# Attention output kept channel-major up to the output product, in a two-part transformer block on one core

## The chip, the cores and the metric

The kernel is one program on one core of a Trainium2 chip. The metric is the device time of a run in microseconds. Three runs of the kernel before gave 793.11, 795.96 and 798.07 us; the time before is their median, 795.96 us.

## What is computed

The block has two residual parts on a sequence of 2048 tokens with 512 channels, all in float32. `mod` is a row of six vectors computed from a condition `c`.

```python
h = layernorm(x) * (1 + ca) + sa
x = x + ga * A(h)
h = layernorm(x) * (1 + cb) + sb
x = x + gb * B(h)

# A: 32 heads of 16 channels, 4 segments of 512 tokens, causal inside a segment
a_dot = softmax(q k^T / 4 + mask) v
a_mem = (phi(q) M) / (phi(q) z + 1e-6)      # M, z: sums over the segments before
o = g * a_mem + (1 - g) * a_dot             # g = sigmoid(beta), one number a head
A = o @ wo
# B: relu(h @ w1 + b1)^2 @ w2 + b2, 1792 hidden channels
```

In the first segment M and z are zero, so its memory part is zero.

## The kernel before

**Units.** Attention is cut into 16 units: unit u is segment s = u // 4 and channel group cc = u % 4, that is 8 heads by 512 tokens. `qk` (L726) makes q and k of a unit, SP copies them into the operand tile ST (`fill`, L797: 12 DMAs a unit), `a_quad` (L850) finds row maxima for 4 heads at a time and SP writes them into ST (`rows`, L933), `b_quad` (L1019) makes the scores, the exponentials and the product with V. `mem` (L941) reads the memory M for segments 1 to 3 and adds to it for segments 0 to 2.

**What leaves a unit.** The product with V leaves each group of four heads in a PSUM bank as channel-major rows: 32 rows a head, of which 16 are channels and the 17th is the softmax denominator (V has a column of ones), by 512 tokens. ScalarE copies each of the two banks of a unit to `oraw` (L1110). `turn_o` (L1117) then turns them on TensorE with 2 x 8 transposes of 64x128 blocks, in two halves with a GpSimd memset between them as a hinge. `norms` (L1135) divides by the denominator and gates by 1 - g on VectorE, token-major. `mem` does the same for the memory part: 8 small products of phi(q) with M (L954), then a gate on VectorE (L957). The sum of both is made on GpSimd (on VectorE in the last segment, L1157). Segments 0 to 2 store it to `o_dram` (L1160); the last segment leaves it in SBUF, in X1L.

**Output product.** `wo_tile(g, ...)` (L1200) handles 128 tokens: it loads the rows of `o_dram` (the last segment reads X1L), turns them back to channel-major with 4 transposes on TensorE (L1219), splits the result in a high part (ScalarE, L1225) and a low part (VectorE, L1227), both out of PSUM, and does 4 steps of 3 matmuls each with `wo` (L1192 to L1194). The residual is added on VectorE (L1234).

**Second part.** `ffn1` and `ffn2` (L1348, L1378) run per segment over 14 blocks of 128 hidden channels. Their weights are loaded and split only when the SBUF of the attention part is free (`open_ffn`, L1300, `load_w1`, `load_w2`). The 16 output tiles are stored by SP (L1396), the last half tile by ScalarE's queue.

**Order.** Nothing is scheduled on the chip. Every operation is a node of a plan, numbered in the order in which the code makes it, and `ORDER` (L57 to L214) holds the node numbers of PE, ACT, DVE, POOL and SP in the order in which each engine runs them. An engine takes its list strictly in turn, and SP issues its DMAs strictly in turn: a DMA whose data isn't ready holds all DMAs behind it in the list. `Plan.run` models durations and ends at the end of TensorE's last node (L374), which is what the lists were made against. The SP list of before ends like this:

```
2710 2735 2696 2728 2717 2738 2731 2724 3162 2957 3575 3373 3364 3367 3168 2963 2960 3569 3370 3159 3578 3165 3572
2954
```

The last 16 are the stores of the output tiles. 2954 to 2963 belong to segment 0, 3159 to 3168 to segment 1, 3364 to 3373 to segment 2 and 3569 to 3578 to segment 3, so the third store of the list is one of segment 3.

Of the kernel before, what the change touches and what calls it, by code (L numbers as in the profile page):

```python
# [8 lines left out]
F32 = mybir.dt.float32  # L9
# [9 lines left out]
P = 128  # L19
# [12 lines left out]
VROW = NB * VA  # L32

# [25 lines left out]
16 48 32 25 76 42 68 73 54 50 19 74 46 56 80 45 69 63 3 77 31 78 40 29 65 62 24 36 17 22 59 47 41 66 71 79 51 43-44 57  # L59
82 21 84 94 102 26 61 96 104 113-114 58 30 125 38 81 126 49 83 67 27 70 35 28 33 72 23 85 178-179 64 39 168 180-181  # L60
169-172 182-183 18 184 173 60 174 75 175 185 34 20 52 55 37 53 333-336 204 338-339 205-206 238 246 207 340 248 341
209-212 257 490-491 243 492-493 270 749-750 495-496 251 759-760 497-498 221-223 276 224 262 253 226 265 227 362
228-229 267 614 281 615 288 291 616 272 617 375 296 619 284 620 381 386 621-622 372 370 300 304 279 301-302 311 367
314 307 391 433 319 377 389 394 519 404 323 436 324-325 438 445 396 406 527 538 412 327 448 767 329 768 441 769-770
532 453 551 772-773 557 548 774-775 524 529 420 457 560 458-459 422 414 461 546 464 428 468 872 471 934-935 534 476
936 543 937 643 656 430 480-482 562 648 939 569 940 681 941 651 942 565 800-801 577 802 553 803 572 484 805-806 486
807 662 808 581 653 585 582-583 592 675 658 588 600 670 595 1344-1345 1354-1355 667 684 604-606 672 686 1005 834 1067
693 1068 696 1069 677 1070 701 847 608 1072 610 689 1073 853 1074 844 1075 875 842 705-707 709 817 712 818 839 819 716
820 866 719 822 861 823 849 724 824 967 825 858 975 728-729 863 881 888 730 878 1200 980 868 1201 972 986 1202-1203
994 884 1205 1138 891 896 1206-1208 977 900 904 991 982 1100 1108 907 901 732 911 734 914 902 1113 919 923 1008 999  # L70
# [1363 lines left out]
```

## Time and profile before

| | |
|---|---|
| time, median of 3 runs | 795.96 us (793.11 to 798.07) |
| profiled execution, its own time | 798.18 us |
| profiled execution, span of the trace | 796.3 us |
| granted TensorE clock, mean | 0.989 |
| attention part | up to about 463 us of the span |
| second part on TensorE | 463 to 784 us |

The span runs from the first to the last instruction of the trace. A row of a timeline gives start and duration in microseconds, engine, line, operation and tile, "output<-input", and the count of instructions that the row merges; in brackets stands idle time before it and what ended it. PE's matmuls overlap, so the time that a group costs TensorE is the distance from its start to the start of the next row, not its duration. SPq is SP's sequencer, which issues DMAs; ACTq is that of ScalarE. A row of a stage table gives for each engine its busy time and count of instructions, then the granted clock as a fraction of the full one, the mean busy share of the 16 DMA engines, and GB/s.

### The profile page before, as it was taken

Reading aid. Unit: us, or ns where it says so; the run is one execution under the profiler, and the core shown is the slowest. Engines: PE = TensorE matmul, PEld = TensorE weight load, DVE = VectorE, ACT = ScalarE, POOL = GpSimd, SP = SyncE. Lnnn points to the kernel's source line nnn. Section 1 sums busy time; section 2 is a strip of 40 time slices with the busy share of each in tenths; the row PEclk is TensorE's granted clock in tenths of the full one; section 3 lists DMA queues with packets and bytes.
Section 4 is the critical chain, followed back from the end, with each engine's and each line's share of the span. In section 5 each row is a group of like instructions: output and inputs, shape, how many; then the busy total and the mean of one; then the engine's idle time right before and its main releaser. Section 6 shows DMA issues by size and latency. Waiting matters only on the chain.

```text
span 796.3 us, 16568 instructions
## 1 busy us (share of the span) xinstructions
PE 769.0 (97%) x6075; PEld 577.9 (73%) x6075; DVE 528.2 (66%) x1493; ACT 430.6 (54%) x908; POOL 222.1 (28%) x334
## 2 busy tenths in 40 slices
PE   8999999999999999999999999999999999999993
PEld 4776657775778658685676678888888888888883
DVE  4777688888998887689798878676522342323232
ACT  2568568879778885779647545433322232222130
POOL 1746454456655784344232200000000000000000
PEclk9999899999999999999999999999999999999998
DMA  8845652333333342453531254320000000000005
GB/s 270 244 102 128 185 178 52 82 82 82 95 91 85 83 95 63 100 119 116 160 102 41 82 147 119 97 62 1 0 1 1 0 27 1 1 0 1 0 1 184
DMA packets 51306, 65.33 MB, mean 82 GB/s; under 512 B 7829, under 2 KB 24985, under 8 KB 51226
## 3 DMA queue, kind: packets, MB, share of 16 engines
q1 hardware_dynamic: 51074, 64.14, 28.9%
q8 instruction: 48, 0.79, 0.4%
q14 instruction: 32, 0.26, 0.1%
q10 hardware_dynamic: 152, 0.13, 0.1%
HBM read 29.91 MB, written 7.34 MB: 47 GB/s over the span
## 4 chain that ended last, share of the span: by engine, by line
PE 66%; ACT 3%; DVE 2%; DMA 2%; SPq 1%; issue 1%; POOL 0%; DVEq 0%; POOLq 0%; ACTq 0%
PE bh L1357 6%; PE bh L1356 6%; PE bh L1358 6%; PE bpf L1385 6%; PE bpf L1386 6%; PE bpf L1384 6%; PE bqk L744 5%; PE bpv L1086 5%; PE bpb L1027 4%; PE ba L857 3%; PE bv L824 3%; ACT pt L1044 2%; PE bwop L1192 2%; PE bwop L1194 2%; PE bwop L1193 1%; PE blnq L606 1%
## 5 line engine op out<-in xcount | busy, mean ns | idle before, releaser
L862 DVE CUSTOM_DVE_ANT_0 ba<-ba,msk 128x384 f32<-128x384 f32 (+2 forms) x384 | 186.3, 543 | 31.2 <-PE ba L857 26.1
L1044 ACT ACTIVATE pt<-bpb 128x512 f32<-128x512 f32 x320 | 173.6, 614 | 30.8 <-PE bpb L1027 29.0
L1373 DVE TENSOR_TENSOR r<-r 128x512 f32<-128x512 f32 x56 | 38.7, 692 | 136.9 <-ACT rr L1370 136.7
L744 PE MATMUL bqk<-HT,WQK 64*128 64x512 f32 x720 | 102.5, 398 | 1.1 <-ACT phi L790 1.1
L1031 POOL TENSOR_SCALAR_AFFINE_SELECT pt<-pt 128x512 f32<-128x512 f32 x128 | 80.4, 646 | 82.9 <-ACT pt L1044 62.8
L1366 ACT ACTIVATE r<-bh,b1c 128x512 f32<-128x512 f32 x56 | 38.5, 688 | 109.6 <-DVE rr L1374 56.5
L1384 PE MATMUL bpf<-W,rr 128*128 128x512 f32 x224 | 88.1, 393 | 0.0
L1385 PE MATMUL bpf<-W,rr 128*128 128x512 f32 x224 | 87.8, 392 | 0.0
L1386 PE MATMUL bpf<-W,rr 128*128 128x512 f32 x224 | 87.7, 392 | 0.0
L1027 PE MATMUL bpb<-ST 64*128 64x256 f32 (+2 forms) x512 | 80.6, 356 | 2.6 <-DMA ST<-mt 1.3
L1086 PE MATMUL bpv<-pt,VT 128*32 128x512 f32 (+3 forms) x1024 | 81.2, 441 | 0.2
L857 PE MATMUL ba<-ST 63*128 63x256 f32 (+2 forms) x512 | 74.4, 344 | 4.1 <-DMA ST<-sg 2.7
L744 PEld LDWEIGHTS bqk<-HT,WQK 64*128 64x128 f32 x720 | 67.0, 186 | 11.2 <-ACT phi L790 1.4
L1370 ACT ACTIVATE rr<-r 128x512 fp32r<-128x512 f32 x56 | 35.4, 632 | 70.7 <-PE bpf L1386 70.1
L1027 PEld LDWEIGHTS bpb<-ST 64*128 64x128 f32 x512 | 50.3, 188 | 23.9 <-ACT pt L1044 5.8
L857 PEld LDWEIGHTS ba<-ST 63*128 63x128 f32 x512 | 49.8, 189 | 22.1 <-ACT pt L1044 7.5
L824 PE MATMUL bv<-WVO,HT 64*128 64x512 f32 x384 | 55.0, 397 | 0.2
L862 DVE DVE_READ_ACCUMULATOR2_ANT mx<- 128x1 f32 x384 | 54.7, 142 | 0.0
L1086 PEld LDWEIGHTS bpv<-pt,VT 128*32 128x32 f32 x1024 | 27.8, 110 | 34.1 <-issue 26.3
L1384 PEld LDWEIGHTS bpf<-W,rr 128*128 128x128 f32 x224 | 42.1, 188 | 9.2
L1385 PEld LDWEIGHTS bpf<-W,rr 128*128 128x128 f32 x224 | 42.1, 188 | 9.1
L1386 PEld LDWEIGHTS bpf<-W,rr 128*128 128x128 f32 x224 | 42.1, 188 | 9.0
(162 smaller groups left out, 1442.2 us busy)
## 6 DMA issues: line engine op xcount, KB each, us to landing
ST<-sg SPq DMA_DIRECT2D x192, 128.0 KB
wr<-in_B_w SPq DMA_DIRECT2D x28, 256.0 KB
wm<-in_w_mod SPq DMA_DIRECT2D x24, 256.0 KB
xt<-in_A_x SPq DMA_DIRECT2D x16, 256.0 KB
xw<-in_A_x SPq DMA_DIRECT2D x16, 256.0 KB
o_dram<-on SPq DMA_DIRECT2D x12, 256.0 KB
ot<-o_dram SPq DMA_DIRECT2D x12, 256.0 KB
out<-X SPq DMA_DIRECT2D x12, 256.0 KB
```

The lines of the kernel that those rows point to most:

```text
L744: m = nc.tensor.matmul(bank(("qk", u, w)), W3(w, k, x, cc * P, (cc + 1) * P)[z], HT[z, y, k], start=(ph == 0 and k == 0 and i == 0), stop= ...
L824: m = nc.tensor.matmul(bank(("v", s, t)), HT[z, x, k, t * P:(t + 1) * P], WVO[z, k, y], start=(ph == 0 and k == 0 and i == 0), stop=(ph == ...
L857: nc.tensor.matmul(dst[:, c0:c0 + n], ST[b:b + 63, 0, sl, qt * P:(qt + 1) * P], ST[b:b + 63, 1, sl, :n], start=True, stop=True)
L862: nc.vector.tensor_tensor_reduce(i, i, msk[:, 512 - n:], scale=1.0, scalar=-3e38, op0=ALU.add, op1=ALU.max, accum_out=o)
L1027: nc.tensor.matmul(dst, ST[b:b + 64, 1, sl, kb * P:(kb + 1) * P], ST[b:b + 64, 0, sl, q0:512], start=True, stop=True)
L1031: nc.gpsimd.affine_select(out=ap, in_=ap, pattern=[[0, ap.shape[1]], [1, P]], compare_op=ALU.is_ge, fill=0.0, base=0, channel_multiplier=-1)
L1044: ns = [act(512, lambda j=j: nc.scalar.activation(buf("PPP"[n], pt)[:, i + j], bank(keys[j]), AF.Exp, scale=0.25), pr[slot] + 0.01 + 0.001 ...
L1086: nc.tensor.matmul(bank(o)[32 * hq:32 * hq + 32, q0:q0 + src.shape[1]], v[:, a:a + 32], src, start=start, stop=stop, tile_position=(0, 32 ...
L1356: nc.tensor.matmul(p, wh, h2[:, 0, k], start=(k == 0), stop=False)
L1384: nc.tensor.matmul(p, rh, FF["W2"][:, f, 0], start=(f == 0), stop=False)
L1385: nc.tensor.matmul(p, rh, FF["W2"][:, f, 1], start=False, stop=False)
L1386: nc.tensor.matmul(p, rl, FF["W2"][:, f, 0], start=False, stop=(f == NF - 1))
```

## The change

The output of a unit stays channel-major. `turn_o`, `norms` and the gate of `mem` go, and `heads_out` comes:

- `oraw` is one tile [128, 2, 512] a unit. One DMA of 512 KB stores it to a DRAM tile `o_raw[u]`. The memory read is now turned round (M is the stationary operand, phi(q) the moving one with 512 tokens), 20 rows a head instead of 17, so that 4 heads are 80 rows; ScalarE copies its two banks to a tile of pool `oraw` and SP stores 320 KB behind the raw rows.
- `load_d` fetches the denominators as [128, 32] tiles (one or two DMAs), VectorE makes the gates there, `store_g` writes them to `o_gate[u]`, and `load_g` fetches each row 16 times, so that a gate stands in every channel's row (256 KB each).
- `load_o` and `load_a` fetch the 128 channel rows of both parts (256 KB each) into slots 0 and 2 of X1L, the gates go to slots 1 and 3; GpSimd multiplies twice and adds once; `OUT` stores 256 KB to `o_turned[s]`. Segment 0 has no memory part: one multiplication, no sum.
- `wo_tile` loads [128 channels, 4, 128 tokens] from `o_turned`, for all segments, and has no transposes; the high part is copied by ScalarE from SBUF, the low part made by GpSimd (VectorE in the last segment). The rows of `wo` are loaded in the order that the new channel order needs.
- `beta` is loaded by four DMAs of single elements, since the gates now are one column for each channel group.
- `open_ffn` no longer waits in the plan for the `heads_out` of the last segment (list `LATE`).
- The plan's costs are changed (a DMA issue 0.47 us or 0.64 to 0.65 us instead of 0.6, others), its end is now the landing of the last DMA, and the five lists are new throughout. `K_*` and the number of warm-up matmuls are as before.

```diff
-        self.end = max(n.at + n.dur for n in self.nodes if n.eng == "PE")
+        self.end = last_done
...
-    o_dram = dram.tile([S, D], F32, name="o_dram")
+    o_turned = [dram.tile([D, L], F32, name=f"o_turned{s}") for s in range(NS)]
+    o_raw = [dram.tile([2 * P + AROW, 512], F32, name=f"o_raw{u}") for u in range(NU)]
+    o_gate = [dram.tile([2, NB, 512], F32, name=f"o_gate{u}") for u in range(NU)]
...
+                    nc.tensor.matmul(bank(bs[r])[:4 * VP, :], MB[z, cc, r * 4 * VP:(r + 1) * 4 * VP], TL[q_][z, :], start=True, stop=True)
...
+            n = [act(512, lambda r=r: nc.scalar.copy(buf("oraw", ar)[:4 * VP, r], bank(bs[r])[:4 * VP, :]), pr[0] + 0.01, after=[n], put=[bs[r]])
+                 for r in (0, 1)]
+            AMN[u] = sp(lambda: nc.sync.dma_start(o_raw[u][2 * P:].rearrange("(r p) n -> p r n", r=2), TL[ar][:4 * VP]), pr[0] + 0.02, 5 << 16, lat=1.2,
+                        after=n, put=[ar])
...
+    def heads_out(u, pr):
...
+        st = sp(lambda: nc.sync.dma_start(raw[0:2 * P].rearrange("(q p) n -> p q n", q=2), TL[r]), pr + 0.01, 1 << 19, lat=1.2,
+                after=[ORW[u, 0], ORW[u, 1]], put=[r])
...
+        def load_d():
+            nc.sync.dma_start(den()[:, 0], rows(0, 2 * P, 32)[:, DH].rearrange("h (i j) -> h i j", j=32))
+            if s:
+                nc.sync.dma_start(den()[:, 1], rows(2 * P, AROW, VP)[:, DH].rearrange("h (i j) -> h i j", j=32))
...
+        def gate():
+            d = den()
+            if s:
+                nc.vector.tensor_scalar(d[:, 1], d[:, 1], EPS_DEN, ge[:, cc:cc + 1], op0=ALU.add, op1=ALU.mult)
+                nc.vector.reciprocal(d, d)
...
+            nc.vector.tensor_scalar(d[:, 0], d[:, 0], omg[:, cc:cc + 1], None, op0=ALU.mult)
...
+        def load_g(i):
+            nc.sync.dma_start(X1L[:, 1 + 2 * i], o_gate[u][i][None, :, :].to_broadcast([DH, NB, 512]))
+
+        def times(k, f, op_):
+            return lambda: nc.gpsimd.tensor_tensor(X1L[:, k], X1L[:, k], X1L[:, f], op=op_)
...
+        OUT[u] = sp(lambda: nc.sync.dma_start(o_turned[s][cc * P:(cc + 1) * P, :], X1L[:, 0]), pr + 0.09, 1 << 18, lat=1.2, after=[m[-1]], **done(0))
...
-                nc.tensor.transpose(bank(b)[:, k * P:(k + 1) * P], src[:, k * P:(k + 1) * P], ident)
...
+            nc.scalar.copy(TL[ot][:, 0], TL[o])
...
+        l = op("DVE" if last else "POOL", 0.6 if last else 1.24, lambda: (nc.vector if last else nc.gpsimd).tensor_tensor(
+            TL[ot][:, 1], TL[o], TL[ot][:, 0].bitcast(F32), op=ALU.subtract), pr + 0.01, after=[h], put=[o])
...
-    N_FFN = op("NIL", 0.0, open_ffn, -20.0, after=list(PL.nodes))
+    N_FFN = op("NIL", 0.0, open_ffn, -20.0, after=[n for n in PL.nodes if n not in LATE])
```

The new SP list ends with the 16 output stores in this order:

```
3454 3249 3451 3252 3448 3243 3038 3044 3041 3246 3457 3047 3656 3662 3653 3659
```

By the numbering of the changed code, 3038 to 3047 are segment 0, 3243 to 3252 segment 1, 3448 to 3457 segment 2, and 3653 to 3662 segment 3, so the four of segment 3 stand last, in the order in which TensorE finishes their tiles.

Around the end of attention the new lists read as follows. After the last product with V (2547 to 2549), TensorE has the 16 steps of the output tiles 8 to 11 and four groups of transposes of the second layer norm, then 9 steps of `ffn1` of blocks 0, 2 and 3, then output tile 13. SP has, from the raw store of the last unit on: 2551 (raw store), 2690 (output tile 11), 2424 (`load_o` of unit 14), 2552 (`load_d`), 2681, 2433 (`OUT` of unit 14), 2556 (`store_g`), 2691, 2554 (`load_a`), 2559 (`load_g`), 2553 (`load_o`), 2557 (`load_g`), 2728 and 2742 (w1 of blocks 0 and 2), 2857, 2562 (`OUT` of unit 15), 2784 and 2749 (w1 of blocks 8 and 3), 2726, and 2856, 2826, 2836 (output tiles 15, 12, 13). For unit 8 SP has 1555 (raw store), four fills, 1364 (`OUT` of unit 7), 1637 (row maxima), 1556 (`load_d`), three fills, 1560 (`store_g`), 1557, 1558 (`load_o`, `load_a`), 1561 (`load_g`), one fill, 1563 (`load_g`).

More of the change, by code (lines that the diff above doesn't have):

```diff
@@ L32 @@
 VROW = NB * VA
+VP = 20
+AROW = NB * VP
 N_WARM = 70
@@ L248, in op @@
         n.lat = self.LAT[eng] if lat is None else lat
-        n.nd, n.act, n.since = nd, act, -9.0
+        n.nd, n.act, n.since = nd, self.ACT.get(mode) if act is None else act, -9.0
         n.outs, n.left, n.seq, n.at = [], 0, len(self.nodes), None
@@ L349, in run @@
                         beat = (beat + 1) % self.RING
-                    free[e] = end
+                    free[e], last_done = end, max(last_done, done)
                     heapq.heappush(ev, (end, k, n, 0))
@@ L479, in block_kernel @@
     PL.held["pad"] = [("pk", PL.pools["pk"].pop(0))]
-    ge = small.tile([P, H], F32, name="ge", bufs=1)
+    ge = small.tile([P, 4], F32, name="ge", bufs=1)
     def silu():
@@ L555, in mm @@
                                  tile_position=(0, 32 * k))
-        n = pe("C", 0.98, mm, pr + 0.02, after=[n_cs] + loads, get=[("#D", b)], put=[k[1] for k in at if k], act=0.6)
+        n = pe("C", 0.98, mm, pr + 0.02, after=[n_cs] + loads, get=[("#D", b)], put=[k[1] for k in at if k])
         t = ("t", "mod", m)
-        MODT[m] = act(512, lambda: nc.scalar.copy(buf("oraw", t), bank(b)), pr + 0.03, after=[n], get=[("oraw", t)], put=[b])
+        MODT[m] = act(512, lambda: nc.scalar.copy(buf("lnf", t), bank(b)), pr + 0.03, after=[n], get=[("lnf", t)], put=[b])
         return t
@@ L608, in ln_transposed @@
         for h in (0, 1):
-            n.append(pe("F", 0.357, lambda h=h: turn(h), pr + 0.001 * h, after=[after[h], *n], get=() if h else [(kind, q) for q in b], act=0.5))
+            n.append(pe("F", 0.357, lambda h=h: turn(h), pr + 0.001 * h, after=[after[h], *n], get=() if h else [(kind, q) for q in b], act=0.55))
         tok = slice(2 * i * P, 2 * i * P + 2 * P)
@@ L666, in ln1 @@
                 st[t].left += 1
-        r = op("DVE", 2.6, lambda: ln_rstd(TL[mv], 4), p_stat + 0.05, after=st)
+        r = op("DVE", 2.16, lambda: ln_rstd(TL[mv], 4), p_stat + 0.05, after=st)
         HTN[s] = []
@@ L1004, in mem @@
                                  pr[2] + 0.03, after=[n], get=[("pk", tm)], put=[b2])
[L1005 removed]
+                MBN[u] = op("POOL", 1.22, lambda: blocks(lambda m, r_: nc.gpsimd.tensor_tensor(m, m, heads(TL[tm][r_, :2 * VA]), op=ALU.add)),
                             pr[2] + 0.04, after=[n, *MRD[u]], put=[tm])
@@ L1108, in b_quad @@
         VUSE[u].append(k)
-        r, b, on = ("oraw", u, qd), ("fin", u, qd), ("on", u)
-        ORW[u, qd] = act(512, lambda: nc.scalar.copy(buf("oraw", r), bank(o)), p_fin, after=[k, ORW.get((u - 1, 1))], get=[("oraw", r)], put=[o])
-        if qd == 0:
-            return
-        last = s == NS - 1
-        tail = []
-        def turn_o(ph):
-            for t in range(4):
-                for r in (0, 1):
-                    z = slice(64 * r, 64 * r + 64)
-                    m = nc.tensor.transpose(bank(("fin", u, ph ^ r))[:, t * P + 64 * r:t * P + 64 * r + 64],
-                                            TL["oraw", u, ph ^ r][z, t * P:(t + 1) * P], ident[z, z])
-                    if ph == 0 and t == 3:
-                        tail.append(m)
-                    if ph and t == 0:
-                        swap(m, tail)
@@ L1239, in ln2 @@
     def ln2(s, pr, wait=()):
-        r = op("DVE", 2.6, lambda: ln_rstd(st_all[:, 4 * s:4 * s + 4], 4), pr[0] - 0.1, after=[X1N[4 * s + t] for t in range(4)] + (XWN if s else []))
+        r = op("DVE", 2.16, lambda: ln_rstd(st_all[:, 4 * s:4 * s + 4], 4), pr[0] - 0.1, after=[X1N[4 * s + t] for t in range(4)] + (XWN if s else []))
         H2N[s] = []
```

464 lines of the change are left out of this document (235 added, 229 removed), and 11 rows, old and new, of the table ORDER.

## The prediction

> **What bounds the kernel now.** I read the page first, then the table by stages, the groups by line and shape, the waits, the timeline of TensorE and of SP, and the chain that ended last.
>
> ```profile
> span 796.3 us, 16568 instructions
> PE 769.0 (97%) x6075; PEld 577.9 (73%) x6075; DVE 528.2 (66%) x1493; ACT 430.6 (54%) x908; POOL 222.1 (28%) x334
> ```
> ```profile
> 60.00:460.00 400.00, 388.36 (x4239) 273.34 (x4236) 336.57 (x1120) 301.39 (x683) 195.62 (x292) 0.99 0.38 102
> 463.00:785.00 322.00, 321.14 (x1425) 262.92 (x1423) 149.84 (x263) 101.11 (x163) 0.00 (x0) 1.00 0.08 24
> 785.00:797.00 12.00, 0.00 (x0) 0.00 (x0) 0.45 (x1) 0.00 (x0) 0.00 (x0) 0.67 0.82 302
> ```
>
> There are three stages with different limits. From 60 to 460 us TensorE is busy for 388 of 400 us: work taken off it there is worth its length, and its waits are 11.6 us in all. From 463 to 785 it is simply full, and the change touches nothing of it. In the last 12 us it does nothing at all, while the DMA engines run at 302 GB/s. That tail is no drain, it is stored-up output:
>
> ```profile
> 783.75 0.39 PE L1386 MATMUL bpf<-W,rr 128*128 128x512 f32 x1
> 784.92 3.41 SPq L1396 DMA_DIRECT2D out<-X  x6
> 792.31 0.53 SPq L1396 DMA_DIRECT2D out<-X  x1
> ```
> ```profile
> SPq L1396 <- DVE X1L L1394: 138.1, 1, 138.1
> ```
>
> The last matmul ends at 784.14, the span 12.2 us later. SP waited 138.1 us for one tile of the last segment, with the finished tiles of the earlier segments (out<-X) behind it in its list.
>
> **The change part by part.**
>
> *Transposes removed.* The busy time of these groups overlaps, so I take distances between starts:
>
> ```profile
> L1121 PE MATMUL bfin<-ident,oraw 64*128 64x64 f32 x256 | 14.6, 231 | 0.3 <-POOL hinge_s L502 0.2
> L1219 PE MATMUL bwot<-ident,ot 128*128 128x128 f32 x48 | 7.6, 282 | 0.0
> L1219 PE MATMUL bwot<-ident,X1L 128*128 128x128 f32 x16 | 2.2, 276 | 0.0
> ```
> ```profile
> 441.19 0.40 PE L1121 MATMUL bfin<-ident,oraw 64*128 64x64 f32 x8
> 441.52 1.07 PE L1086 MATMUL bpv<-pt,VT 128*32 128x384 f32 x16
> ...
> 442.86 0.41 PE L1121 MATMUL bfin<-ident,oraw 64*128 64x64 f32 x8
> 443.08 0.54 PE L1027 MATMUL bpb<-ST 64*128 64x256 f32 x4
> ...
> 444.12 0.66 PE L1219 MATMUL bwot<-ident,ot 128*128 128x128 f32 x4
> 444.70 1.11 PE L954 MATMUL bmr<-MB,phi 64*128 64x68 f32 x16
> 445.62 0.82 PE L1027 MATMUL bpb<-ST 64*128 64x256 f32 x8
> ...
> 449.80 2.36 PE L1086 MATMUL bpv<-pt,VT 128*32 128x512 f32 x32
> 452.09 0.50 PE L1192 MATMUL bwop<-WVO,oT 128*128 128x512 f32 x1
> ...
> 462.67 0.60 PE L1219 MATMUL bwot<-ident,X1L 128*128 128x128 f32 x4
> 463.02 0.48 PE L1356 MATMUL bh<-H2a,W 128*128 128x512 f32 x1
> ```
>
> A group of 8 (bfin) costs 0.22 us among scores and 0.33 next to a product with V; 256 instructions are 32 groups, 7.0 to 10.6 us; I take 0.29, 9.3 us. A group of 4 (bwot) costs 0.35 to 0.58; 16 groups are 5.6 to 9.3 us; I take 0.44, 7.0 us. Together -16.3 us, all on the path.
>
> *Memory read turned round.* Before, 16 instructions took 0.92 us (444.70 to 445.62). The new form isn't in the trace. Nearest is the product with V, also plain float32 on a part of the array: 32 instructions in 2.29 us, four side by side, so 8 lengths that add up to twice 1280 columns; 512 columns in two passes are 2 x 512 / 2560 x 2.29 = 0.92 us. If the two row halves run side by side the read costs the same, 0; if they don't, 0.92 more for 12 units, +11 us. All other row-half products of this kernel come in pairs that overlap, so I take 0.
>
> *Tail.* The stores of segments 0 to 2 now stand before those of segment 3, and the list follows the order in which the tiles end. After the last matmul remain an add, one issue and one landing. A landing under load follows from 792.31: the issue ends at 792.84, the span 3.5 us later, with other stores in front and the end of the program in it. So 0.2 + 0.69 + 0.5 + 3.5 = 4.9 us in place of 12.2: -7.3 us. With the landing of a load below (2.34 us) it is -8.4; with two more stores of 0.9 us in front, -5.5.
>
> *The way through DRAM, and the end of attention.* This is the part that costs. Prices of a hop (issues of fills and row maxima on SP's queue as shortest/median/longest ns; a load's issue, and what waits for it; the landing of two row DMAs):
>
> ```profile
> L799 SPq DMA_DIRECT2D ST<-sg x192: 607/608/1806, 31.8 to 399.8; - x192
> L935 SPq DMA_DIRECT2D ST<-mt x64: 626/680/911, 59.4 to 438.8; - x64
> ```
> ```profile
> 467.32 0.37 SPq L1322 DMA_DIRECT2D wr<-in_B_w  x1
> ```
> ```profile
> 470.03 0.62 ACT L1324 CAST W<-wr 128x512 fp32r<-128x512 f32 x1 [1.88 <-DMA wr<-in_B_w]
> ```
> ```profile
> 321.44 2.10 DMA ST<-mt
> ...
> 387.67 3.36 DMA ST<-mt
> ```
> ```profile
> L1157 POOL TENSOR_TENSOR on<-on,am 128x512 f32<-128x512 f32 x8 | 10.3, 1285 | 3.5 <-DVE on L1151 3.5
> ```
> ```profile
> L963 DVE RECIPROCAL den<-den 128x16 f32<-128x16 f32 x24 | 6.1, 253 | 0.8
> L1325 DVE TENSOR_TENSOR W<-wr,W 128x512 fp32r<-128x512 f32 x14 | 9.5, 687 | 3.5 <-ACT W L1324 3.5
> ```
>
> 256 KB land 2.34 us after the end of their issue (467.69 to 470.03), and at 280 GB/s (my round value between the 302 of the tail and 102 / 0.38 = 268 of the attention stage) each further 256 KB in front adds 0.9. A pair of 4 KB transfers takes 2.1 us from its first issue (once 3.4). Count from the end of the last product with V. ScalarE's copy and semaphores: 0.9. Raw store: issue 0.5, landing 2.3 + 0.9, at 4.7. `load_d`: two issues, 0.6 each, 1.5 to land, at 7.4. Gate on [128, 64]: 0.9 (the reciprocal has four times 16 elements), at 8.4. `store_g`: 0.5 + 1.5, at 10.4. SP stood still for it; now it issues two gate loads and `load_o`, and only then, at 11.7, w1 of block 0. That is the fourth transfer of 256 KB in the line: landed at 15.8, split by ScalarE (0.62) and VectorE (0.69) with semaphores by 17.6.
>
> TensorE has until then 16 steps of the output product and four transpose groups:
>
> ```profile
> 458.82 0.50 PE L1194 MATMUL bwop<-WVO,oT 128*128 128x512 f32 x1 [0.38 <-DVE oT L1227]
> 459.16 0.40 PE L1192 MATMUL bwop<-WVO,oT 128*128 128x512 f32 x1
> ...
> 459.86 0.40 PE L1192 MATMUL bwop<-WVO,oT 128*128 128x512 f32 x1
> ```
>
> A step is 0.70 us (459.16 to 459.86), a transpose group 0.44: 16 x 0.70 + 4 x 0.44 = 13.0 us. It waits 17.6 - 13.0 = 4.6 us for block 0. Next late: `OUT` of unit 15 holds SP until three GpSimd operations of 1.29 us are through (17.8), so w1 of block 3 goes out at 19, lands third in its line at 22.3 and is split by 24.1, where TensorE arrives five steps after 17.6, at 21.1: 3.0 us. Output tile 13 comes out of `OUT` (lands 20.5) and three loads at 27.4, 0.6 us late. Behind these waits stands all of the second part. In all 8.2 us, against the 0.4 us of the row at 458.82 before. Bounds: 3 us if SP gets to w1 of block 0 two hops' spread (1.3 us each) sooner and block 3 is then in time, 15 us if every hop has the 3.36 of the slow row.
>
> A wait of that length has a second price:
>
> ```profile
> 90.00:92.00 2.00, 2.00 (x14) 0.34 (x10) 0.00 (x0) 0.00 (x0) 0.00 (x0) 0.50 0.27 91
> ...
> 182.00:184.00 2.00, 2.00 (x19) 0.72 (x20) 1.83 (x9) 1.64 (x4) 0.26 (x1) 0.50 0.00 0
> ```
> ```profile
> PE bmod L554 <- DMA wm<-in_w_mod: 1.8, 1, 1.8
> PE bat L927 <- DVE sg L783: 0.9, 1, 0.9
> ```
>
> The granted clock is at half after a wait of 1.8 us (at 88 to 90) and of 0.9 us (at 180); the slices around these show it for about 3.4 us, so 1.7 us lost each time. I add 1.7 once; the 3.0 us wait could cost it again, which stays inside the bounds. The transition is +8.2 + 1.7 - 0.4 = +9.5 us.
>
> If the clock drops came with the transposes instead, taking them out would give back at most the (1 - 0.99) x 400 = 4 us that the stage row shows lost; I count nothing for it, since both slices follow waits. The Trainium skill ("TensorE: Matmul & The Clock Gate", "Part 4: PE-mode transpose") speaks for the other side: transposes don't count as busy time for the clock. By that the sum would end up to 4 us lower; no row here shows it.
>
> *The rest of attention.* VectorE loses the norms, the memory gate and the low part of 12 output tiles; GpSimd gains three operations of 1.29 us a unit and 12 low parts, some 60 us on 196 of 400. Neither sets the end of this stage. SP gains up to ten issues a unit, and a unit with memory moves 512 + 320 + 256 KB of stores, 256 + 256 + 512 KB of loads and 64 KB of small things, one without 1312 KB: 12 x 2176 + 4 x 1312 KB, less 12 stores of 256 KB, plus 4 loads in the last segment, are 29 MB more. At 268 GB/s these are 110 us of all engines, so the DMA share goes from 0.38 to about 0.65. I take 0 for this: what falls away (waits on VectorE, hinges) against what comes (waits on SP). Ends: -5 (half of the 11.6 us of waits go) and the first rival's price.
>
> **Sum.** -16.3 + 0 - 7.3 + 9.5 + 0 = -14.1 us. Of the profiled execution's 798.18 us (span 796.3 and 1.9 around it) that leaves 784.1; the median shown is 2.2 us below that execution, so the forecast is 795.96 - 14.1 = 781.9 us, 1.8% less. Its own range, from the bounds of the transition and of the transposes, is 776 to 788.
>
> **Rivals.**
>
> *SP becomes the bound of attention (slower).*
>
> ```profile
> PE ba L857 <- DMA ST<-sg: 2.7, 3, 1.6
> ```
>
> A unit issues 12 fills and 4 row DMAs, 12 x 0.61 + 4 x 0.68 = 10.0 us of its 25 (400 us by 16). The change adds about 5 us of issues and blocks SP at `store_g` and `load_g`: in unit 8 by 3.0 us (landing and gate) less 1.8 for the three fills between, and 2.0 less 0.8 for two loads, some 2.4 us. 17 of 25 us still fit. But TensorE already waited for fills three times, and fills can't go out before their tiles are free, so a blocked SP can pass 2.5 us of the 7 a unit on to TensorE: 11 units x 2.5 = +27.5, 795.96 - 14.1 + 27.5 = 809 us. It decides from 1.3 us a unit. Against it: SP is idle for most of the time, and TensorE waited only 2.7 us for it.
>
> *The hops are slow.* If the chain at the end goes by the 3.36 us row, the transition costs 15 + 1.7 - 0.4 = 16.3 in place of 9.5: 789 us. For it speaks the higher DMA share, against it that little else moves at that point.
>
> *The transition is covered and attention's waits shrink.* With the lower bound of 3 us, 1.7 of clock gone too, and -5 of waits: -16.3 - 7.3 + 3 - 0.4 - 5 = -26, 770 us. For it speaks that VectorE, busy for 337 of 400 us, gets lighter.
>
> *The turned read doesn't pair.* Then it does more TensorE work than it is meant to: -14.1 + 11 = -3.1, 793 us.
>
> *The clock of attention comes back.* If the drops came with the transposes, the 4 us worked out above from the 0.99 of the stage row go too: 778 us. Against it stand the two slices at half clock.
>
> **How the numbers follow.** Forecast 0.41, clock back 0.05, covered transition 0.20, slow hops 0.16, unpaired read 0.05, SP bound 0.13. About 1% (8 us) can be told from no change here. Faster by over 1%, below 788: the forecast, the clock, the covered case and a part of the slow hops, 0.70. Within 1%: the rest of the slow hops and the unpaired read, 0.17. Slower: 0.13. The range 769 to 797 leaves out the SP case and a little below.
>
> **What would show it.** Right: no bfin and bwot in the trace; after the last matmul at most 6 us; the read at about 0.9 us per unit; TensorE idle for some 4 us ahead of the first step of `ffn1`, released by ScalarE or VectorE behind a w1 load, and again ahead of block 3; a half clock after it; the stage from 463 as long as before. Wrong: waits of `ba` and `bpb` for DMA of more than 10 us in all, the stage up to the last product with V longer than 452 - 10 us, or a tail that is still over 8 us.

## The result, and the profile after

The changed kernel takes 814.37 us (median of 4 runs, 813.71 to 814.9), the kernel before beside it 794.77 (793.11 to 798.07). The ratio is 1.0241, with a 95% interval of 1.0203 to 1.0279: 2.4% slower. The forecast was 781.9 us in a range of 769 to 797. The profiled execution took 814.87 us with a span of 813.1 us, 16.8 more than the span of before.

The page of the changed kernel, then its table by stages (columns as in the prediction: busy time of PE, PEld, DVE, ACT, POOL, then granted clock, DMA share, GB/s):

```profile
span 813.1 us, 15766 instructions
PE 767.9 (94%) x5611; PEld 563.7 (69%) x5611; DVE 500.6 (62%) x1353; ACT 441.5 (54%) x932; POOL 274.8 (34%) x362
```
```profile
60.00:460.00 400.00, 374.69 (x3771) 252.40 (x3767) 297.89 (x963) 306.88 (x702) 243.62 (x316) 0.98 0.60 167
460.00:500.00 40.00, 30.01 (x105) 22.78 (x104) 22.56 (x37) 13.48 (x23) 6.30 (x5) 0.83 0.62 172
500.00:802.00 302.00, 302.00 (x1330) 244.97 (x1329) 139.04 (x248) 94.14 (x151) 0.00 (x0) 1.00 0.09 28
```

TensorE's busy time fell by 1.1 us, from 769.0 to 767.9, with 464 matmuls less. Its idle time between 60 and 460 us went from 11.6 to 25.3 us, and the 40 us behind that now have a clock of 0.83. The second part from 500 us on is as full as before.

The timeline of TensorE in the changed kernel, at the landmarks:

```profile
445.96 2.36 PE L1090 MATMUL bpv<-pt,VT 128*32 128x512 f32 x32
...
456.86 0.66 PE L620 MATMUL blnq<-ident,xh 128*128 128x128 f32 x4 [1.63 <-DVE xh L611]
463.14 0.63 PE L620 MATMUL blnq<-ident,xh 128*128 128x128 f32 x4 [2.39 <-DVE xh L611]
473.68 0.50 PE L1383 MATMUL bh<-H2a,W 128*128 128x512 f32 x1 [4.47 <-ACT W L1351]
481.89 0.79 PE L1383 MATMUL bh<-H2a,W 128*128 128x512 f32 x1 [2.66 <-ACT W L1351]
...
808.98 0.39 PE L1413 MATMUL bpf<-W,rr 128*128 128x512 f32 x1
```

The last product with V is over at 448.3 (2.29 us after its start, as before), against 452.1. The last matmul ends at 809.4, against 784.1. So the difference of the spans has three parts: attention -3.8 us, from there to the last matmul 361.1 in place of 332.0, which is +29.1, and the tail 3.7 in place of 12.2, which is -8.5.

Part of the +29.1 is work that the new lists moved there. The table below takes idle time and lost clock apart, from slices of 2 us: idle time is length less busy time, lost clock is busy time times (1 - granted clock), and the rest is called work. Lost clock is thus an estimate from the granted clock of each slice. The idle time can be read from two rows a kernel, up to the last product with V and from there to 540 us. Before:

```profile
0.00:452.10 452.10, 437.52 (x4592) 307.13 (x4592) 368.25 (x1207) 326.11 (x739) 222.04 (x333) 0.99 0.43 116
452.10:540.00 87.90, 87.31 (x412) 71.41 (x409) 68.90 (x137) 39.13 (x67) 0.09 (x1) 1.00 0.34 96
```

and after:

```profile
0.00:448.30 448.30, 419.10 (x4108) 283.22 (x4108) 324.20 (x1037) 330.30 (x752) 262.98 (x353) 0.98 0.61 171
448.30:540.00 91.70, 79.46 (x328) 62.21 (x326) 67.76 (x137) 35.62 (x60) 11.80 (x9) 0.93 0.51 146
```

| | before | after | difference |
|---|---|---|---|
| idle up to the last product with V | 14.6 | 29.2 | +14.6 |
| idle from there to 540 us | 0.6 | 12.2 | +11.6 |
| lost clock in both | 4.8 | 14.3 | +9.5 |
| tail | 12.2 | 3.7 | -8.5 |
| rest: work of TensorE | 764.1 | 753.7 | -10.4 |
| span | 796.3 | 813.1 | +16.8 |

So 26.2 us of waits and 9.5 us of lost clock ate 10.4 us of removed work and 8.5 us of tail. The waits of TensorE before 448 us, grouped:

```profile
PE bwarm L546 <- POOL msk L433: 4.2, 1, 4.2
PE bpv L1090 <- POOL pt L1035: 4.0, 6, 1.6
PE bpb L1031 <- DVE mx L876: 3.2, 3, 1.8
PE bpb L1031 <- DMA ST<-mt: 2.5, 4, 1.1
PE ba L871 <- DMA ST<-sg: 1.9, 2, 1.3
...
PE bqk L758 <- POOL hinge_s L510: 1.7, 1, 1.7
```

There is no one large wait. The fills (`ST<-sg`), for which the first rival would have TensorE wait, are not the largest. One chain of the changed kernel shows what stands behind such a wait (the chain that ended last, in order of time):

```profile
247.00 3.59 DMA o_gate<-den
250.65 3.80 DMA X1L<-o_gate
254.52 1.26 POOL X1L L1176
255.86 1.66 PE bqk L758 x12
```

The gates are stored (3.59 us) and loaded again (3.80); GpSimd stands in front of its multiplication for 5.2 us, and the one-element memset that lets TensorE go on with `qk` comes after it in GpSimd's list. On SP's queue the same round trip shows as (waits up to 448 us: line, what released it, total, times, longest):

```profile
SPq L1170 <- DVE den L1166: 15.3, 8, 5.2
...
SPq L1173 <- DMA o_gate<-den: 8.0, 7, 2.0
SPq L1191 <- POOL X1L L1176: 7.8, 6, 5.2
```

The queues moved 94.15 MB in place of 64.14 (queue, packets, MB, share of 16 engines), first before, then after:

```profile
q1 hardware_dynamic: 51074, 64.14, 28.9%
```
```profile
q1 hardware_dynamic: 76338, 94.15, 40.8%
```

### The profile page after: what moved, and what is told of

Same layout as the page of the kernel before. It is cut to its first block, busy times and chain, and to the rows that moved or that the text cites. A ratio compares the mean times of both kernels' runs of the same rounds, so it can differ in the third digit from the quotient of the medians.

```text
span 813.1 us, 15766 instructions
## 1 busy us (share of the span) xinstructions
PE 767.9 (94%) x5611; PEld 563.7 (69%) x5611; DVE 500.6 (62%) x1353; ACT 441.5 (54%) x932; POOL 274.8 (34%) x362
## 3 DMA queue, kind: packets, MB, share of 16 engines
q1 hardware_dynamic: 76338, 94.15, 40.8%
## 4 chain that ended last, share of the span: by engine, by line
PE 68%; DMA 10%; DVE 7%; ACT 6%; SPq 4%; issue 3%; POOL 2%; ACTq 0%; DVEq 0%; POOLq 0%
PE bh L1383 6%; PE bh L1385 6%; PE bh L1384 6%; PE bpf L1412 6%; PE bpf L1411 6%; PE bpf L1413 6%; PE bqk L758 5%; PE bpv L1090 5%; PE bv L838 4%; PE bpb L1031 4%; PE ba L871 4%; SPq L813 2%; PE bwarm L546 2%; DMA ST<-sg 2%; PE blnq L620 1%
## 5 line engine op out<-in xcount | busy, mean ns | idle before, releaser
L876 DVE CUSTOM_DVE_ANT_0 ba<-ba,msk 128x128 f32<-128x128 f32 (+2 forms) x384 | 186.1, 542 | 65.1 <-PE ba L871 52.5
L1048 ACT ACTIVATE pt<-bpb 128x512 f32<-128x512 f32 x320 | 170.0, 609 | 22.4 <-PE bpb L1031 18.3
L758 PE MATMUL bqk<-HT,WQK 64*128 64x512 f32 x720 | 100.4, 396 | 1.7 <-POOL hinge_s L510 1.7
L1090 PE MATMUL bpv<-pt,VT 128*32 128x512 f32 (+3 forms) x1024 | 84.7, 456 | 4.5 <-POOL pt L1035 4.0
L871 PE MATMUL ba<-ST 63*128 63x256 f32 (+2 forms) x512 | 81.6, 356 | 3.4 <-DMA ST<-sg 1.9
L758 PEld LDWEIGHTS bqk<-HT,WQK 64*128 64x128 f32 x720 | 70.6, 185 | 12.0 <-POOL hinge_s L510 2.2
L871 PEld LDWEIGHTS ba<-ST 63*128 63x128 f32 x512 | 53.3, 189 | 26.9 <-issue 7.0
L1176 POOL TENSOR_TENSOR X1L<-X1L 128x512 f32<-128x512 f32 x40 | 51.5, 1292 | 42.8 <-DMA X1L<-o_gate 28.9
L1383 PE MATMUL bh<-H2a,W 128*128 128x512 f32 x112 | 46.1, 412 | 7.1 <-ACT W L1351 7.1
L1411 PEld LDWEIGHTS bpf<-W,rr 128*128 128x128 f32 x224 | 42.1, 188 | 9.7
```

Of the source, the lines that this page charges most:

```text
L758: m = nc.tensor.matmul(bank(("qk", u, w)), W3(w, k, x, cc * P, (cc + 1) * P)[z], HT[z, y, k], start=(ph == 0 and k == 0 and i == 0), stop= ...
L871: nc.tensor.matmul(dst[:, c0:c0 + n], ST[b:b + 63, 0, sl, qt * P:(qt + 1) * P], ST[b:b + 63, 1, sl, :n], start=True, stop=True)
L876: nc.vector.tensor_tensor_reduce(i, i, msk[:, 512 - n:], scale=1.0, scalar=-3e38, op0=ALU.add, op1=ALU.max, accum_out=o)
L1048: ns = [act(512, lambda j=j: nc.scalar.activation(buf("PPP"[n], pt)[:, i + j], bank(keys[j]), AF.Exp, scale=0.25), pr[slot] + 0.01 + 0.001 ...
L1090: nc.tensor.matmul(bank(o)[32 * hq:32 * hq + 32, q0:q0 + src.shape[1]], v[:, a:a + 32], src, start=start, stop=stop, tile_position=(0, 32 ...
L1383: nc.tensor.matmul(p, wh, h2[:, 0, k], start=(k == 0), stop=False)
```

## The experiments

Three theories of what attention lost. *Round trip*: SP and GpSimd take their lists in turn and stand at a hop (`store_g`, `load_g`, a multiplication) with fills, masks and hinges behind them. *GpSimd's time*: 40 operations of 1.29 us in place of 8 (the expectation below counts 44), which delay masks and slow VectorE. *Traffic*: 30 MB more make every landing later. For the transition: w1 stands behind the round trip of unit 15 in *SP's order*. Gains over the changed kernel are differences of ratios times 795 us, since the kernel before was run again beside each group of experiments (796.6, 795.5, 797.4 and 796.3 us). By the intervals of the two ratios each such gain is good to about 4 us, so gains that differ by less are not told apart. Positions and waits are those of one profiled execution a kernel.

**All round-trip waits cut.**

```diff
-            nc.sync.dma_start(den()[:, 0], rows(0, 2 * P, 32)[:, DH].rearrange("h (i j) -> h i j", j=32))
+            nc.sync.dma_start(den()[:, 0], xs[0:NB].rearrange("h (i j) -> h i j", j=32))
...
-            nc.sync.dma_start(X1L[:, 1 + 2 * i], o_gate[u][i][None, :, :].to_broadcast([DH, NB, 512]))
+            nc.sync.dma_start(X1L[:, 1 + 2 * i], xs[NB * i:NB * i + NB][None, :, :].to_broadcast([DH, NB, 512]))
```

The loads of the two parts are changed in the same way, and the gate store takes its data from a constant.

> The changed kernel, in which the denominators, both parts and the gates are loaded from rows of the input x in place of DRAM tiles just written, and the gate store takes its data from a constant: all DMAs and operations stay, with the same sizes, only their waits for one another's landings go (the attention output is therefore not the attention's). Round-trip theory (SP and GpSimd stand in order behind landings): the last product with V ends 15 to 25 us earlier, at 423 to 433, and the two waits of the transition shrink, 785 to 797 us. Theory of GpSimd's time and theory of traffic: the last product with V moves by less than 6 us, and only the transition gains, 803 to 812 us.

807.29 us, ratio 1.0134 (1.0101 to 1.0167): 8.5 us gained.

```profile
437.58 2.36 PE L1090 MATMUL bpv<-pt,VT 128*32 128x512 f32 x32
...
466.20 0.79 PE L1383 MATMUL bh<-H2a,W 128*128 128x512 f32 x1 [6.13 <-ACT W L1351]
```

The last product with V ends at 439.9, 8.4 us earlier: more than the other theories allow, half of what the round trip alone should give. The transition's idle time stayed, at 13.0 us in place of 12.2; its largest wait even grew from 4.47 to 6.13 us, although unit 15's loads no longer wait for what was stored. So the waits for the round trip are a part of attention's loss, and not the cause of the transition's.

**GpSimd without the gate.**

```diff
-        m = [op("POOL", 1.24, times(0, 1, ALU.mult), pr + 0.07, after=[lg[0], l[1]], **done(1))]
+        m = [op("POOL", 1.24, times(0, 0, ALU.mult), pr + 0.07, after=[lg[0], l[1]], **done(1))]
```

> The changed kernel, in which GpSimd multiplies each part with itself in place of its gate (the output isn't gated): GpSimd no longer waits for the landing of a gate load, SP still stands at the gate store. The cut of all round-trip waits brought the last product with V 8.4 us forward. If these were GpSimd's (masks and hinges behind a multiplication whose gate hasn't landed), 5 to 8 us come back here, 440 to 443; if they were SP's (fills and row maxima behind the gate store), less than 3.

808.58 us, ratio 1.0156 (1.0122 to 1.0191): 6.8 us gained. The product with V ends at 444.4, 3.9 us earlier, between the two marks; the waits for masks went from 4.0 to 1.0 us and that for the hinge, 1.7 us, is gone. By that mark GpSimd's place behind the gate is about half of the round trip's price (3.9 of 8.4 us), by the time it is more (6.8 of 8.5); the runs don't settle the share.

**GpSimd's operations short.**

```diff
-            return lambda: nc.gpsimd.tensor_tensor(X1L[:, k], X1L[:, k], X1L[:, f], op=op_)
+            return lambda: nc.gpsimd.tensor_tensor(X1L[:, k, 0:8], X1L[:, k, 0:8], X1L[:, f, 0:8], op=op_)
```

> The changed kernel, in which GpSimd's multiplications and additions of the heads work on 8 of 512 tokens (so most of the attention output stays without its gate): 44 operations of 1.29 us become short, all waits stay. Theory of GpSimd's time (these operations slow VectorE, and hinges and masks stand behind them): the last product with V ends 12 to 25 us earlier, and the small operations of the layer norm on VectorE go back from 229 and 290 to about 163 ns; 790 to 802 us. Round-trip and traffic theories: it moves by less than 6 us, and the transition gains up to 3 us; 806 to 813 us.

805.76 us, ratio 1.0119 (1.0081 to 1.0156): 9.7 us gained, but where they came from the trace can't say. The product with V ends at 447.9 in the profiled execution, which is the longest of the four (809.78, with 13.5 us of lost clock); its idle time is 4.1 us shorter, 26.7 and 10.6.

VectorE's small operations stayed slow, so the multiplications aren't what slows them (L608, mean of the 8 up to 440 us: 308 ns, 286 in the changed kernel, 163 over the whole of before). That mean is one operation, beside a product of GpSimd (L807) that the kernel before has too:

```profile
225.05 1.28 DVE L608 SCALAR_TENSOR_TENSOR lny<-lnt,lny 128x4 f32<-128x4 f32 x1
```
```profile
225.02 1.29 POOL L807 TENSOR_TENSOR phi<-phi,e 128x512 f32<-128x512 f32 x1
```

So up to 440 us it is a matter of when the two meet, and not a new operation. Behind the last product with V it is the other work that GpSimd got, the low part of the output tiles. GpSimd and VectorE there, in this run:

```profile
449.63 1.30 POOL L1254 TENSOR_TENSOR oT<-ot,oT 128x512 fp32r<-128x512 f32 x1 [2.45 <-DMA xw<-in_A_x]
```
```profile
449.45 0.16 DVE L607 TENSOR_TENSOR lnt<-lnt,lnv 128x4 f32<-128x4 f32 x1
449.64 1.30 DVE L608 SCALAR_TENSOR_TENSOR lny<-lnt,lny 128x4 f32<-128x4 f32 x1
```

An operation on 128x4 numbers that takes 0.16 us elsewhere takes 1.30, as long as GpSimd's low part beside it. The Trainium skill ("SBUF — State Buffer", "Who interferes with whom") says that a VectorE instruction with two SBUF inputs contends with a GpSimd instruction that reads SBUF, and that the shared ports are an exclusive lock; the trace agrees, with 1.30 us in place of 0.16.

**Fewer bytes, all hops kept.**

```diff
-            nc.sync.dma_start(X1L[:, 0], rows(0, 2 * P, 32)[:, 0:DH, :].rearrange("h e n -> e h n"))
+            nc.sync.dma_start(X1L[:, 0, 0:16], rows(0, 2 * P, 32)[:, 0:DH, 0:16].rearrange("h e n -> e h n"))
...
-            nc.sync.dma_start(X1L[:, 1 + 2 * i], o_gate[u][i][None, :, :].to_broadcast([DH, NB, 512]))
+            nc.sync.dma_start(X1L[:, 1 + 2 * i, 0:16], o_gate[u][i][None, :, 0:16].to_broadcast([DH, NB, 16]))
```

> The changed kernel, in which the loads of both parts and of the gates fetch 16 of 512 columns (14.3 MB of the 29 MB added go; number and order of the DMAs and all waits stay; most of the attention output is therefore stale). Theory of traffic (the added bytes make every landing later): the last product with V ends 5 to 10 us earlier than 448.3 and the landings of 256 KB at 468 and 476 us fall from 5 to under 4 us; 800 to 808 us. Round-trip theory (it is the number of hops in a row, not their size): less than 3 us, above 810.

801.54 us, ratio 1.0070 (1.0038 to 1.0103): 13.6 us gained, by the medians the largest gain of a single cut. The ten runs spread from 796.05 to 806.09, and the profiled execution is the shortest of them, so its positions show more than the median gained.

```profile
432.32 2.36 PE L1090 MATMUL bpv<-pt,VT 128*32 128x512 f32 x32
```
```profile
0.00:434.60 434.60, 413.49 (x4104) 286.15 (x4107) 324.52 (x1039) 330.68 (x752) 263.58 (x353) 0.99 0.54 148
434.60:540.00 105.40, 96.65 (x414) 76.44 (x411) 83.04 (x174) 44.96 (x75) 11.76 (x9) 0.95 0.41 117
```

The product with V ends 13.7 us earlier; idle time is 21.1 and 8.8 us, lost clock 8.0 in place of 14.3. The same chain as above in this kernel:

```profile
241.00 3.40 DMA o_gate<-den
244.47 2.41 DMA X1L<-o_gate
```

The store of 32 KB, whose size is as before, hardly changed (3.59 to 3.40 us); the load of the gates, 8 KB in place of 256, lands after 2.41 in place of 3.80. So at this hop the gain is the load's own size; that the bytes delay other transfers has to be shown elsewhere (the 512-column run below). The edit takes 14.2 MB out, half of the added bytes. A point of the expectation failed: of the two w1 landings in the transition one fell from 5.38 to 3.10 us, the other stayed at 4.69.

**The three cuts together.** No other edit than those shown.

> The changed kernel with the three cuts together: loads from the input in place of what was just written, GpSimd's operations on 8 of 512 tokens, loads of 16 of 512 columns (the output isn't the attention's). If these three hold all that attention lost, the 14.8 us of TensorE waits and 3.2 us of clock more than before go, and the last product with V ends at about 430. If a part lies in the new order of the five lists itself (waits for VectorE's row maxima at 227 and 282, the longer start), it stays above 436, and the time at 798 to 806.

793.60 us, ratio 0.9963 (0.9934 to 0.9992): 22.1 us gained.

```profile
429.82 2.36 PE L1090 MATMUL bpv<-pt,VT 128*32 128x512 f32 x32
```

The product with V ends at 432.1, near the 430 of "these hold all". Idle time up to it is 19.5 us, 4.9 above before. Among what stays are two that stand in the lists: the start (4.2 in place of 2.1 us for `msk`, which GpSimd makes behind clears of V and M), and waits for VectorE's row maxima (3.2 us in the changed kernel, 4.3 here). The single gains (8.5, 9.7 and 13.6) don't add up to 22.1; one hop's wait can go by fewer bytes or by a cut chain.

**Issues and bytes on the kernel before.** DMAs that nobody waits for, 16 and then 512 columns wide:

```diff
+            if u < 12:
+                for j in (0, 1):
+                    k = 2 * qd + j
+                    nc.sync.dma_start(X1L[:, k, 0:16], xs[k * P:(k + 1) * P, 0:16])
+                    nc.sync.dma_start(extra[4 * u + k][:, 0:16], WVO[:, k, 0].bitcast(F32)[:, 0:16])
```

> The kernel before, with four more DMAs behind each pair of row-maxima DMAs of units 0 to 11 (two loads from x into slots that are free until the last segment, two stores of a weight to DRAM tiles that nothing reads), 16 columns each: 96 more issues on SP, nearly no bytes, and no operation waits for them. By SP's time (22 DMAs of about 0.6 us in a unit of 25 us) nothing happens: within 2 us of before. If SP's issues were what attention lost, 3 to 8 us more.

> The same 96 DMAs on the kernel before with 512 columns, 256 KB each, 25 MB in all (the change added 29 MB): bytes without any hop that waits for them. If bytes cost by themselves, since fills and row maxima land later behind them, TensorE's waits for DMA grow from 4 us to 8 or more and the time by 4 to 10 us over the same kernel with 16 columns. If bytes cost only through the hops that stand in order behind each other, under 2 us.

816.87 us, ratio 1.0236 (1.0200 to 1.0273), with 16 columns, and 826.61 us, 1.0343 (1.0305 to 1.0381), with 512. The first was a surprise: four issues of 0.47 us behind each pair of row maxima, nearly no bytes, cost 18.8 us. A part of the chain that ended last with 16 columns, then a fill of the chain with 512 columns:

```profile
265.73 0.43 SPq L941
266.20 2.60 DMA ST<-sg
```
```profile
273.04 4.25 DMA ST<-sg
```

and two waits of TensorE with 16 columns:

```profile
76.98 1.28 PE L858 MATMUL ba<-ST 63*128 63x512 f32 x2 [4.37 <-ACT pt L1050]
...
305.37 0.92 PE L858 MATMUL ba<-ST 63*128 63x256 f32 x6 [3.08 <-DMA ST<-sg]
```

With 16 columns the fills of that chain land as fast as before (2.60 and 2.69 us; 2.27 to 2.74 in the kernel before), but they go out behind the added issues. 24 blocks of 1.9 us on SP are 45.6 us, of which 12.3 arrive as idle time of TensorE and 6.3 as lost clock. SP has slack on average, yet at the places where the fills follow the row maxima it has no 1.9 us to spare.

The bytes cost 8.5 us on top (1.0343 - 1.0236), 0.35 us for each of 24.4 MB, without a hop that waits for them. The fills land later (2.60 to 4.25 us in the chain), and TensorE's waits for fills (`ST<-sg`) and loads (`wm`) grew from 5.6 to 11.3 us. So bytes cost by themselves. In the changed kernel 14.2 MB cost 13.6 us, 0.96 for each, which is more; how much more is open, with 4 us of error in each, and the two runs move their bytes at different places.

**The transition: w1 earlier.** First with blocks 0 and 2 ahead of the gate store of unit 15 and block 3 ahead of 8 (a part of SP's list, here and below):

```diff
-2556 2691 2554 2559 2553 2557 2728 2742 2857 2562 2784 2749
+2691 2728 2742 2556 2554 2559 2553 2557 2857 2749 2562 2784
...
```

> The changed kernel, with the loads of w1 of blocks 0 and 2 put ahead of the gate store of unit 15 in SP's list, and that of block 3 ahead of the store of unit 15's output. Theory of SP's order at the end of attention: the waits of 4.5 and 2.7 us ahead of blocks 0 and 3 go, and with them most of the 6.8 us of clock lost from 460 to 500 us: 8 to 13 us less than the changed kernel, 801 to 806. Rival: the waits only move to what is now later in the list (output tiles 12 to 15), then under 4 us less, above 810. The stage up to the last product with V stays at 448 us by both.

818.06 us, ratio 1.0257 (1.0226 to 1.0289): nothing gained. The wait ahead of block 0 went from 4.47 to under 0.5 us, but ScalarE splits block 8 ahead of block 3, and block 8 now came last:

```profile
486.28 0.79 PE L1383 MATMUL bh<-H2a,W 128*128 128x512 f32 x1 [10.19 <-ACT W L1351]
```

So this order of the two blocks is a fault of its own; the same with 8 ahead of 3:

```diff
+2691 2728 2742 2556 2554 2559 2553 2557 2857 2784 2749 2562
...
```

> The changed kernel, with w1 of blocks 0 and 2 behind the x rows of tile 11 and ahead of unit 15's gate store, and blocks 8 and 3, in that order, ahead of unit 15's output store; the x rows still wait for a free load buffer. With the load buffers also freed, the transition lost 4 us less than in the changed kernel. If the place in SP's list is the cause, the same 4 to 7 us here, 807 to 810 us; if the load buffer is, 1 us or less, 813 and above.

815.88 us, ratio 1.0227 (1.0192 to 1.0262): 1.1 us, within the error.

```profile
469.87 0.50 PE L1383 MATMUL bh<-H2a,W 128*128 128x512 f32 x1 [1.48 <-ACT W L1351]
...
480.43 0.80 PE L1383 MATMUL bh<-H2a,W 128*128 128x512 f32 x1 [5.93 <-ACT W L1351]
487.96 0.80 PE L1222 MATMUL bwop<-WVO,oT 128*128 128x512 f32 x1 [2.82 <-ACT oT L1252]
```

3.0 us ahead of block 0 turned into 3.3 more ahead of block 3 and 2.8 ahead of output tile 13. By its expectation this is the outcome in which the load buffer, not the place in the list, is the cause. But it is a weak test of the place: w1 of block 0 still stands behind the x rows of output tile 11, which wait for a free load buffer, and went out at 466.00, 14.9 us after the last product with V, in place of 467.77, 19.5 us after it. Then with free load buffers, and w1 ahead of unit 14's output store (2433) too:

```diff
-            nc.sync.dma_start(buf("xr", xk), xs[g * P:(g + 1) * P, :])
+            nc.sync.dma_start(buf("xr", xk) if last else x1(g), xs[g * P:(g + 1) * P, :])
...
-2552 2681 2433 2556 2691 2554 2559 2553 2557 2728 2742 2857 2562 2784 2749
+2552 2681 2691 2728 2742 2433 2556 2554 2559 2553 2557 2857 2784 2749 2562
...
```

> The changed kernel, with the x rows of output tiles 0 to 11 loaded to where the sum is written, so that they wait for no free load buffer, and with the loads of w1 of blocks 0 and 2 right behind the x rows of tile 11, ahead of unit 14's output store and of unit 15's gate store; blocks 8 and 3 ahead of unit 15's output store. Theory of SP's order (w1 stands behind what waits): block 0 starts at most 20 us after the last product with V in place of 25.4, the waits ahead of blocks 0 and 3 are under 3 us in all, 800 to 806 us. Rival: the layer norm on VectorE or the way of tile 11 holds TensorE next, less than 4 us gained, above 810.

809.90 us, ratio 1.0165 (1.0131 to 1.0200): 6.0 us gained.

```profile
454.99 0.98 SPq L1349 DMA_DIRECT2D wr<-in_B_w  x2
```

w1 goes out 9.5 us after the last product with V. Block 0 starts 19.9 us after the last product with V, as expected, without a wait, but 2.33 us follow inside it for VectorE's split of w1 and 2.44 ahead of block 3: more than the 3 allowed. The transition's idle time is 8.7 us in place of 12.2. The edit frees the buffers and moves w1 at once, so it doesn't say which of the two did it. With all cuts on top:

> The three cuts of attention (loads from the input, GpSimd on 8 of 512 tokens, 16 of 512 columns; the output isn't the attention's) together with the freed load buffers and the earlier w1 of the transition. The three cuts alone took 22 us off the changed kernel, the transition alone 6. If the two losses are separate, they add up: 28 us off, 786 to 788 us beside 796 of before, and from the last product with V to 540 us TensorE waits under 5 us in place of 12.2. If the transition's loss was only what the late round trips left behind, the sum stays at that of the three cuts, 792 to 795.

792.74 us, ratio 0.9951 (0.9928 to 0.9974), 1.0 us better than without the earlier w1, within the error: the second outcome. Idle time behind the last product with V is 7.4 us against 7.9. So hardly anything of the 6.0 us is left once the three cuts are made. Of these the cut waits had left the transition's idle time at 13.0 us and the fewer bytes took it to 8.8, so by these traces it is the bytes rather than the waits of the round trip that the transition shares with attention. Why 7 to 8 us stay is not shown; in all these runs the loads for output tiles, w1 and unit 15 go through one SP list and two split buffers, and a load that moved forward moved another back.

**The tail alone.** The kernel before with one edit (SP's list from 2724 on):

```diff
-2724 3162 2957 3575 3373 3364 3367 3168 2963 2960 3569 3370 3159 3578 3165 3572
-2954
+2724 2954 2957 2960 2963 3159 3162 3165 3168 3364 3367 3370 3373 3569 3575 3578 3572
```

> The kernel before, with only the last 16 output stores in SP's list put in the order in which TensorE ends their tiles (segments 0, 1, 2, then 3). If the tail of before is stored-up output behind one late store, as the prediction has it, the span after the last matmul falls from 12.2 us to 3.7 to 6, as in the changed kernel, and the time by 6 to 8.5 us, to 786 to 789. If the DMA engines were the limit there (302 GB/s), the tail stays above 10 us and the time within 2 us of before.

787.64 us (785.39 to 792.01), ratio 0.9892 (0.9842 to 0.9942): 8.6 us less than before (4.6 to 12.6 by the interval), the fastest kernel of this study.

```profile
780.43 0.39 PE L1385 MATMUL bpf<-W,rr 128*128 128x512 f32 x1
```

The last matmul ends at 780.8, the span at 785.4: 4.6 us of tail in place of 12.2.

## Why the prediction was wrong

The sum of the prediction against the profiled executions, term by term:

| term | forecast | measured |
|---|---|---|
| transposes and read | -16.3 + 0 | -10.4 |
| tail | -7.3 | -8.5 |
| transition: waits and lost clock | +9.5 | +17.9 (11.6 + 6.3) |
| rest of attention: waits and lost clock | 0 | +17.8 (14.6 + 3.2) |
| sum | -14.1 | +16.8 |

- *The rest of attention.* "I take 0 for this" is the step that failed: 17.8 of the 30.9 us between forecast and measured. It put no price on a DMA share that it had itself worked out at 0.65 (0.60 measured) and 29 MB more (30.0 measured), nor on SP and GpSimd standing at the hops. Attention's waits grew by 14.6 us, and its clock loss by 3.2. The single cuts give 13.6 us for half of the bytes and 8.5 for the chain, 22.1 in all with GpSimd's operations, the transition's share included. How the 22.1 us divide among the three stays open.
- *The first rival* had the sign, and at 809 us came nearest to the time, with a chance of 0.13. Its mechanism was a part: the cut chain gave 8.5 of its 27.5 us. It looked at fills only; its mark, waits of `ba` and `bpb` for DMA above 10 us, stayed at 4.4, though the stage up to the last product with V did stay above 442 us (448.3). What it did not see is GpSimd, which stands at the gate just as SP does, with masks and hinges behind it, and the bytes. "SP is idle for most of the time" was no argument: on the kernel before, 1.9 us in the wrong place cost 0.8.
- *Transition.* Mis-sized, by 8.4 us. The waits ahead of blocks 0 and 3 were 4.47 and 2.66 us, forecast 4.6 and 3.0, but that they agree is luck: w1 of block 0 went out 19.5 us after the last product with V in place of 11.7, and TensorE was through with its output steps after 20.9 in place of 13.0. SP's order did hold block 0; with w1 moved forward its wait fell to under 0.5, 1.48 and 0 us. It did not set the length of the transition, since the waits came back ahead of block 3 and output tile 13. The forecast missed 4.5 us of waits for VectorE's layer norm (`blnq`). In the trace of the changed kernel two of its operations on 128x4 numbers take 1.22 us each beside GpSimd's low parts (at 451.37 and 452.62), and unit 15's gate stands ahead of a later step in VectorE's list; no run moved either, so this cause is read and not shown. The clock term was 6.3 us in place of 1.7, since the clock fell to half at each of the three long waits (2.39, 4.47 and 2.66 us), not once.
- *Tail.* -8.5 in place of -7.3, right, and shown alone: 12.2 to 4.6 us.
- *Transposes and read.* No `bfin` and `bwot` are left, and the read costs what was forecast. A read of the changed kernel with what follows it, then row maxima (`ba`) of the same size without a read in front:

```profile
217.44 1.02 PE L964 MATMUL bmr<-phi,MB 64*80 64x512 f32 x4
217.90 0.86 PE L871 MATMUL ba<-ST 63*128 63x256 f32 x4
218.69 1.06 PE L1090 MATMUL bpv<-pt,VT 128*32 128x512 f32 x8
```
```profile
316.75 0.45 PE L871 MATMUL ba<-ST 63*128 63x256 f32 x4
317.04 0.45 PE L1031 MATMUL bpb<-ST 64*128 64x256 f32 x4
```

Read and row maxima take 1.25 us together. Such row maxima take 0.29 us here, mostly 0.39 to 0.48 ahead of a product with V, so 0.8 to 1.0 us are the read's, 0.92 before. The rule of the profile section, that a group costs the distance to the next row's start, gives 0.46 us for it, half of that: the next group starts beside the read and ends late. TensorE's work should have fallen by 16.3 us; it fell by 10.4, and hardly more in the run with all cuts (10.9). The measure is good to about 3 us: up to the last product with V it gives 432.7 us before and 429.9 with the 16-column DMAs, which have the same work on TensorE. An estimate of what may hide in it: the first product after a wait counts 0.50 us as busy where the next ones add 0.23 (473.68, then 477.90 to 478.13 at full clock), 0.27 us a wait, and the trace lists 50 waits of over 0.15 us in place of 21, 7.8 us. But the kernel with all cuts has 33 waits and no less work (753.2 us), so where the missing 5.9 us are stays open.

- *Clock back.* With the transposes gone attention lost 8.0 us of clock in place of 4.8, beside 14.6 us more waits, so these 4 us did not come back; whether transposes had a part in the drops can't be told.
- *Range.* The prediction's own range, 776 to 788, is that of the transition alone (3 and 15 us give 777 and 789); with the 12.6 to 19.9 us of the transposes it is 773 to 792.

## What to carry to other kernels

A way through DRAM is priced by three things, not by its time: by what stands behind each of its waits in the list of each engine that takes part, by its bytes, which make other transfers land later (fills 4.25 us in place of 2.60), and by the half clock that some of its waits bring (9.5 us more lost here). A queue's mean load says nothing of its slack at one place: put a probe there before you count on it. When you price a group of matmuls by the distance to the next start, look at the end of the next group too. When a change contains an independent repair (here the order of the last stores), make that alone first.

## What the runs showed of the hardware

- An operation of GpSimd on 128x512 numbers in SBUF stretched a VectorE operation on 128x4 numbers with two SBUF inputs beside it to its own length: 0.16 us became 1.28 to 1.30.
- Half clock follows some waits and not others. In the changed kernel it came at waits of 1.79 us (at 282), 2.39, 4.47 and 2.66, and not after 1.68 (at 255.86) and 1.63 (at 456.86). How much is lost differs between runs of nearly the same instructions: up to the last product with V 8.0 us in the changed kernel, 14.4 and 8.2 in the two kernels that differ from it only behind that point (w1 earlier, without free load buffers).
- Loads of 8 KB against 256 KB, same hop: 2.41 against 3.80 us to land; a store of 32 KB took 3.4 to 3.6 us in both.
- Four products of a 64x80 block with 512 float32 columns, two on each row half, cost TensorE 0.8 to 1.0 us, though the next group starts after 0.46 us.
